# Low parts of decoded weights on VectorE, one-bank accumulators, and a later decode of one weight pair

## The chip, the cores and the metric

The kernel runs on one core of one Trainium2 chip. The metric is the device time of one execution in microseconds (us); lower is better. TensorE is called PE here, its weight loads PEld, VectorE DVE, ScalarE ACT, GpSimd POOL and SyncE, which issues the DMAs, SP. The times in the rows below count from the start of the span.

## The reference, cut to what matters

Three layers follow each other. The first is attention over a window of 64 positions (4 batches, 8 heads, 576 positions, 64 wide). The second mixes its output by a Fourier transform over positions and channels, normalises, and applies a two-layer network; the third is a gated network.

```python
X = np.fft.fft(np.fft.fft(x, axis=1), axis=2)
u = x + np.real(X)
un = (u - mean) / sqrt(var + 1e-6)
y = u + np.maximum(un @ w_ch1, 0) @ w_ch2          # 512 -> 2048 -> 512
h = gelu_tanh(y @ w_in); a, v = halves of h        # 512 -> 2 x 512
out = y + (a * (w_sg @ layernorm(v) + b_sg)) @ w_out
```

Everything is float32. The kernel multiplies in a faster format and keeps the precision by splitting each factor into a high and a low part: one product is three matmuls (`mm3`, L119 to L126: high by high, high by low, low by high).

## The kernel before, in words

**Decoding weights.** The weights arrive as raw 64-bit floats and are turned into float32 on the core, in pieces of 128x256. One piece (`raw`, L150 to L162) is a DMA on SP, one ACT instruction (L158, into `dec_g`) and three DVE instructions (L159, L160, L161, into `dec_w`). `halves` (L164 to L166) then splits a decoded piece: ACT copies the rounded value into the high part (L165), and POOL subtracts it from the piece to give the low part (L166). The parts go into one of nine buffers `set0` to `set8`. L166 runs 103 times in the program.

**The plain stage** (`mlp`, L636 to L683, about 156 to 350 us). The 2304 positions are cut into six chunks of 384, and the hidden layer into sixteen slices of 128. Six of the slices are computed plainly, in 36 blocks of one slice and one chunk. A block's first product gives `h` (12 matmuls, two buffers); ACT makes the high part of its ReLU, `rh` (L670), and DVE the low part, `rl` (L671). Two blocks later the second product (`second`, L642 to L657, 12 matmuls) adds into `acc`, one tile of four banks of PSUM. After a chunk's last slice four DVE additions (L656), one for each bank, move `acc` into the residual `uT`, and the next chunk takes the same tile.

**The seven-product stage** (`wino`, L870 to L912, about 348 to 588 us) computes the other ten slices, in pairs, by a scheme that needs seven products in place of eight. `decode_w1` (L180 to L204) decodes a pair's first weights and forms their sums and differences on DVE (L189, L194, L197, L202); `decode_w2` decodes its second weights. `tees(p)` (L694 to L726) forms the sums and differences of the activations and writes them to memory; `pump` loads them back. `quad` (L775 to L826) makes the seven products, each in a PSUM bank (`w`, six buffers, or `g`, two), and adds them up: DVE where a bank is read, POOL for two additions between SBUF tiles (`u<-u` and `u<-pq,u`, both L799). The two POOL additions stand before the DVE addition `pq<-w,pq`, which releases a bank. L792 (ACT) and L793 (DVE) make the ReLU's parts, and `units` (L828 to L857) does the second products, which L845 adds to `uT`. The first two products of the very first quad are issued early, inside the plain stage.

**What follows.** `split_x` (L864 to L868) splits the result into parts for the gated layer: 24 copies on ACT (L867) and 24 subtractions on POOL (L868).

**What sets the order.** The program is written as generators. `drive` takes work for PE from the main one and fills in pieces of side work from "lanes": decodes, norms, `tees`. A scheduler then places the instructions on each engine in an order of its own, by its own model of when each one could run, and an edit in one place can move instructions in many. Two helpers steer it. `high_priority(URGENT)` favours the instructions that release a bank. `behind(gen)` (L1178 to L1188) and the splitting at L1261 to L1265 place work after the instructions in `k.marks`, the last ReLU instructions named so far. `pair(6, G6)`, L1230, is the decode of the first pair of slices, 6 and 7; it is added to a lane when the second half of the chunks begins.

`k.bp` is the buffer pool of the plain and the seven-product stage. It is set in `open_mlp` (L622) and set to None at L1266.

Of the kernel before, what the change touches and what calls it, by code (L numbers as in the profile page):

```python
# [9 lines left out]
F32 = mybir.dt.float32  # L10
# [3 lines left out]
ALU = mybir.AluOpType  # L14
# [93 lines left out]
class Kernel:  # L108
# [54 lines left out]

    def halves(self, f, hi, lo):  # L164
        self.nc.scalar.activation(out=hi, in_=f, func=AF.Copy)  # L165
        self.nc.gpsimd.tensor_tensor(out=lo, in0=f, in1=hi, op=ALU.subtract)  # L166

    def decode(self, src, hi, lo, n=512):
        for o in range(0, n, 256):
# [466 lines left out]
    def mlp(self, before, last):  # L636
        nc = self.nc
        V, A = nc.vector, nc.scalar
        pend = []
        st = {}  # L640

        def second(g, n, f, rh, rl):  # L642
            t = self.sets[f % 8]
            start, size = CHUNKS[n]
            first, last = f == PHASES[g][0][0], f == PHASES[g][0][-1]
            if first:
                st["acc"] = self.bps.tile([128, 4, 512], F32, tag="acc", name="acc")
            acc = st["acc"]
            for c in range(4):
                s = slice(128 * c, 128 * c + 128)  # L650
                self.mm3(acc[:, c, 0:size], [(t[:, 2, s], t[:, 3, s], rh, rl)], first=first, last=last)
            if last:
                with self.tc.high_priority(URGENT):
                    for c in range(4):
                        x = self.uT[:, c, start:start + size]
                        v = V.tensor_tensor(out=x, in0=acc[:, c, 0:size], in1=x, op=ALU.add)  # L656
                self.marks = [v.ins]  # L657

        for g, (fs, ns) in enumerate(PHASES):
            for n in ns:  # L660
                before(g, n)
                xh, xl, size = self.xh[n], self.xl[n], CHUNKS[n][1]
                for f in fs:
                    t = self.sets[f % 8]
                    ps = self.bps.tile([128, 512], F32, tag="h", bufs=2, name="h")
                    o = ps[:, 0:size]
                    self.mm3(o, [(t[:, 0, 128 * k:128 * k + 128], t[:, 1, 128 * k:128 * k + 128], xh[:, k], xl[:, k]) for k in range(4)])
                    rh, rl = self.rpair(3)
                    with self.tc.high_priority(URGENT):
                        a = A.activation(out=rh, in_=o, func=AF.Relu)  # L670
                        v = V.scalar_tensor_tensor(out=rl, in0=o, scalar=0.0, in1=rh, op0=ALU.max, op1=ALU.subtract)  # L671
                        self.marks = [a.ins, v.ins]
                    pend.append((g, n, f, rh, rl))
                    yield 5 * size
                    if len(pend) > 2:
                        second(*pend.pop(0))
                        yield 5 * size
        while pend:
            second(*pend.pop(0))
            if last is not None:  # L680
                last()
                last = None
            yield 1500  # L683
# [91 lines left out]
    def quad(self, s, f, last, early=False):  # L775
# [2 lines left out]
        V, G, A = nc.vector, nc.gpsimd, nc.scalar  # L778
        self.nq += 1
        p1, p5, c11, u3 = self.ptiles[self.nq % 2], *self.ptiles[2:]  # L780
        out = {}

        def mm(i, o):
            hi, lo = self.w1_block(f, i)
# [5 lines left out]
        def relu(e, t, c, eng):  # L790
            rh, rl = self.rfree.pop(0)
            i = A.activation(out=rh, in_=c, func=AF.Relu)  # L792
            j = eng.scalar_tensor_tensor(out=rl, in0=c, scalar=0.0, in1=rh, op0=ALU.max, op1=ALU.subtract)  # L793
            out[e, t] = rh, rl
            return [i.ins, j.ins]

        hp = lambda: self.tc.high_priority(URGENT)
        copy = lambda o, i: A.activation(out=o, in_=i, func=AF.Copy)  # L798
# [1 line left out]
        for i in range(7):  # L800
            o = (self.gtile() if early and i < 2 else self.wps.tile([128, 512], F32, tag="w", name="w"))[:, 0:384]
            mm(i, o)
            with hp():
                if i == 0:
                    copy(p1, o)
                elif i == 1:
                    add(V, c11, o, p1)
                    relu(0, 0, c11, V)
                elif i == 2:
                    add(V, p1, o, p1)  # L810
                elif i == 3:
                    add(V, u3, o, p1)
                elif i == 4:
                    c21 = o
                elif i == 5:
                    copy(p5, o)
                    g = add(G, p1, p1, p5)
                    add(G, p5, u3, p5)
                    relu(1, 1, p5, V)
                    add(V, u3, c21, u3)  # L820
                    relu(1, 0, u3, V)
                else:
                    add(V, p1, o, p1)
                    self.marks = [*relu(0, 1, p1, V), g.ins]
            yield 960
        self.r[s, f] = out  # L826

# [250 lines left out]
def emit(tc, aps):  # L1078
    with ExitStack() as ctx:
# [142 lines left out]
        def before(g, n):  # L1222
            while n not in done:
                next(rest_)
            if n == PHASES[g][1][0]:
# [1 line left out]
                if g == 1:  # L1227
                    lanes[2].append(when(behind(blocks1()), lambda: 3 in done))
                elif g == 2:
                    lanes[1].append(pair(6, G6))  # L1230
                    lanes[2].append(behind(blocks()))
                elif g == 3:
                    drain(lanes[0], lanes[2])
                    lanes[1].append(pair(8, G8))
                    lanes[2].append(raws2())
# [107 lines left out]
```

## Time and profile before

| | before |
|---|---|
| median of 3 runs | 808.35 us (807.84 to 809.95) |
| profiled execution | 807.96 us, of which the span is 806.2 us |
| mean granted clock of TensorE | 0.979 |
| PE busy | 766.3 us (95%) |
| DVE busy | 526.2 us (65%) |
| ACT busy | 342.7 us (43%) |
| POOL busy | 288.5 us (36%) |

A busy time is the part of the span in which the engine worked on some instruction. "A <- B" in a row on waits means that an instruction of A stood still until B ended. The granted clock, PEclk, is a share of TensorE's full speed; 1.00 is 2.4 GHz, and 0.50 is 1.2 GHz.

### The profile page before, as it was taken

The numbers are of one execution on the slowest core, as the hardware profiler recorded it, in microseconds if no ns is written. First come the engines' busy times: TensorE is split into PE (matmuls) and PEld (weight loads), VectorE is DVE, ScalarE is ACT, GpSimd is POOL, SyncE is SP. The second block draws the span as 40 slices with busy tenths as digits, with TensorE's granted clock in tenths as the row PEclk, the third lists the DMA queues.
The fourth block names the chain that finished last, engine by engine and source line by source line (L and its number), as shares of the span: only waits on it lengthen the run. The fifth ranks groups of instructions, "written<-read, shape, count | busy, mean of one in ns | idle before, by whom it ended". The sixth has DMA issues, their size and how long they took to land.

```text
span 806.2 us, 13754 instructions
## 1 busy us (share of the span) xinstructions
PE 766.3 (95%) x5018; PEld 733.3 (91%) x5018; DVE 526.2 (65%) x1131; ACT 342.7 (43%) x807; POOL 288.5 (36%) x351
## 2 busy tenths in 40 slices
PE   7989699899999999979998999999899999999998
PEld 6879588798999989979998999999899998989898
DVE  4878959797377547885559866764760258674762
ACT  4877687664335544341224323331652243130310
POOL 2144535563433547245734412421692020010000
PEclk9999789999999999999999999999999999999999
DMA  8996662252205568538553970962240020204023
GB/s 263 333 266 181 178 192 73 70 168 83 100 27 188 193 218 296 192 127 337 192 221 115 354 288 5 388 249 110 72 136 1 1 67 1 80 11 147 1 79 117
DMA packets 84771, 123.36 MB, mean 153 GB/s; under 512 B 24416, under 2 KB 61664, under 8 KB 84704
## 3 DMA queue, kind: packets, MB, share of 16 engines
q1 hardware_dynamic: 82912, 119.13, 44.2%
q0 software_dynamic: 576, 2.97, 1.1%
q8 instruction: 39, 0.64, 0.3%
q10 hardware_dynamic: 1216, 0.39, 0.2%
q14 instruction: 28, 0.23, 0.1%
HBM read 91.79 MB, written 30.67 MB: 152 GB/s over the span
## 4 chain that ended last, share of the span: by engine, by line
PE 72%; DVE 14%; DMA 4%; ACT 4%; issue 3%; POOL 1%; SPq 0%; DVEq 0%; ACTq 0%; POOLq 0%
PE c L124 6%; PE c L125 6%; PE c L126 6%; PE g L124 6%; PE w L124 6%; PE g L126 5%; PE w L125 5%; PE w L126 5%; PE g L125 5%; PE sc L315 3%; DVE dec_w L160 2%; DVE dec_w L159 2%; PE acc L125 2%; PE acc L126 2%; PE h L124 2%
## 5 line engine op out<-in xcount | busy, mean ns | idle before, releaser
L166 POOL TENSOR_TENSOR set<-dec_w,set 128x256 fp32r<-128x256 f32 x103 | 82.9, 819 | 109.5 <-ACT set L165 86.2
L573 POOL TENSOR_TENSOR rq<-rq,mhalf 128x1 f32<-128x1 f32 (+1 forms) x24 | 16.8, 698 | 158.7 <-DVE rq L572 156.4
L158 ACT ACTIVATE dec_g<-dec_s 128x256 f32<-128x256 f32 x88 | 38.0, 436 | 69.6 <-DVE dec_w L160 31.1
L165 ACT ACTIVATE set<-dec_w 128x256 fp32r<-128x256 f32 x103 | 40.8, 413 | 62.4 <-DVE dec_w L161 29.8
L160 DVE SCALAR_TENSOR_TENSOR dec_w<-dec_g,dec_w 128x256 int32<-128x256 int32 x88 | 51.1, 584 | 1.9 <-ACT dec_g L158 0.6
L124 PE MATMUL acc<-rh,set 128*128 128x384 f32 x144 | 49.4, 343 | 2.7 <-DVE uT L656 1.7
L323 ACT ACTIVATE s<-s,mx 128x128 f32<-128x128 f32 x144 | 46.1, 391 | 11.0 <-DVE mx L321 10.9
L125 PE MATMUL acc<-rl,set 128*128 128x384 f32 x144 | 49.5, 344 | 0.0
L126 PE MATMUL acc<-rh,set 128*128 128x384 f32 x144 | 49.0, 340 | 0.0
L315 PE MATMUL sc<-k,q 128*128 128x128 f32 x288 | 41.9, 296 | 7.1 <-DVE s L318 4.0
L161 DVE SCALAR_TENSOR_TENSOR dec_w<-dec_s,dec_w 128x256 int32<-128x256 int32 x88 | 46.3, 532 | 0.4
L315 PEld LDWEIGHTS sc<-k,q 128*128 128x128 f32 x288 | 38.5, 209 | 8.5 <-DVE s L318 4.4
L159 DVE TENSOR_SCALAR dec_w<-dec_s 128x256 int32<-128x256 int32 x88 | 40.6, 467 | 7.1 <-DMA dec_s<-in_wo 2.8
L1004 DVE BATCH_NORM_STATS2 st<-u 128x6 f32<-128x512 f32 x18 | 12.4, 691 | 45.2 <-ACT u L1000 45.2
L799 DVE TENSOR_TENSOR u<-w,u 128x384 f32<-128x384 f32 x44 | 24.2, 550 | 26.6 <-POOL u L799 17.7
L318 DVE SCALAR_TENSOR_TENSOR s<-sc,mask 128x512 f32<-128x512 f32 x36 | 24.5, 683 | 25.3 <-PE pt L330 15.0
L799 POOL TENSOR_TENSOR u<-u 128x384 f32<-128x384 f32 x15 | 15.5, 1032 | 59.8 <-ACT u L798 42.1
L845 DVE TENSOR_TENSOR uT<-g,uT 128x384 f32<-128x384 f32 x36 | 19.2, 550 | 25.3 <-PE g L126 25.3
L656 DVE TENSOR_TENSOR uT<-acc,uT 128x384 f32<-128x384 f32 x48 | 23.4, 546 | 14.1 <-PE acc L126 14.0
L671 DVE SCALAR_TENSOR_TENSOR rl<-h,rh 128x384 fp32r<-128x384 f32 x36 | 19.6, 550 | 19.1 <-ACT rh L670 18.8
L343 PEld LDWEIGHTS pv<-v,pts 128*64 128x64 f32 x576 | 24.7, 148 | 7.3 <-issue 6.0
L124 PEld LDWEIGHTS acc<-rh,set 128*128 128x128 f32 x144 | 27.5, 191 | 4.0 <-DVE uT L656 2.4
(357 smaller groups left out, 2664.3 us busy)
## 6 DMA issues: line engine op xcount, KB each, us to landing
dec_s<-in_w SPq DMA_DIRECT2D x64, 256.0 KB, 2.8
v<-in_v SPq DMA_DIRECT2D x16, 520.0 KB, 5.2
xht<-xb SPq DMA_DIRECT2D x10, 768.0 KB, 8.1
xhm<-xb SPq DMA_DIRECT2D x10, 768.0 KB, 6.9
xlm<-xb SPq DMA_DIRECT2D x8, 768.0 KB, 8.1
k<-in_k SPq DMA_DIRECT2D x11, 512.0 KB, 6.7
xf<-u SPq DMA_DIRECT2D x18, 256.0 KB, 2.7
p<-xf SPq DMA_DIRECT2D x24, 192.0 KB, 2.7
```

The lines of the kernel that those rows point to most:

```text
L124: mm(out, lhsT=lh, rhs=rh, start=first and i == 0, stop=False)
L125: mm(out, lhsT=lh, rhs=rl, start=False, stop=False)
L126: mm(out, lhsT=ll, rhs=rh, start=False, stop=last and i == n - 1)
L158: nc.scalar.activation(out=g, in_=s[:, :, 1].bitcast(F32), func=AF.Copy, scale=2.0 ** -112)
L159: nc.vector.tensor_scalar(out=w, in0=s[:, :, 0], scalar1=29, scalar2=None, op0=ALU.logical_shift_right)
L160: nc.vector.scalar_tensor_tensor(out=w, in0=g[:].bitcast(I32), scalar=3, in1=w, op0=ALU.logical_shift_left, op1=ALU.bitwise_or)
L161: nc.vector.scalar_tensor_tensor(out=w, in0=s[:, :, 1], scalar=-2147483648, in1=w, op0=ALU.bitwise_and, op1=ALU.bitwise_or)
L165: self.nc.scalar.activation(out=hi, in_=f, func=AF.Copy)
L166: self.nc.gpsimd.tensor_tensor(out=lo, in0=f, in1=hi, op=ALU.subtract)
L315: nc.tensor.matmul(sc[:, hp], lhsT=q[:, hp].rearrange("p a b -> p (a b)"), rhs=k[:, hp, o:o + 128], start=True, stop=True)
L323: nc.scalar.activation(out=s[:, hp], in_=s[:, hp], func=AF.Exp, bias=mx[:, hp:hp + 1])
L799: add = lambda eng, o, i, j: eng.tensor_tensor(out=o, in0=i, in1=j, op=ALU.add)
```

## The change

It has four parts, and the line numbers here are those of before.

1. **Low parts** (L166): where `self.bp` is set, the subtraction is issued on DVE and not on POOL. That holds for 83 of the 103; the other 20 (12 during attention, 8 at the end) stay.
2. **Banks** (L647 to L656): `acc` becomes four tiles of one bank each, with a tag each, `acc0` to `acc3`. The second product's groups and the four additions use one tile each, in place of a quarter of one.
3. **Marks of a quad** (L781 to L824): `self.marks` after a quad names the instructions of all four ReLUs and the first POOL addition. Before, it named those of the last ReLU that is written and that addition. `tees(2)` (L1251) and `split_x` (L1261) are placed behind these marks.
4. **Pair 6** (L1230): its decode goes through `behind`, so that each of its steps is placed after the marks that stand when it is first taken.

```diff
--- before.py
+++ after.py
@@ -163,7 +163,7 @@
 
     def halves(self, f, hi, lo):
         self.nc.scalar.activation(out=hi, in_=f, func=AF.Copy)
-        self.nc.gpsimd.tensor_tensor(out=lo, in0=f, in1=hi, op=ALU.subtract)
+        (self.nc.gpsimd if self.bp is None else self.nc.vector).tensor_tensor(out=lo, in0=f, in1=hi, op=ALU.subtract)
 
     def decode(self, src, hi, lo, n=512):
         for o in range(0, n, 256):
@@ -644,16 +644,16 @@
             start, size = CHUNKS[n]
             first, last = f == PHASES[g][0][0], f == PHASES[g][0][-1]
             if first:
-                st["acc"] = self.bps.tile([128, 4, 512], F32, tag="acc", name="acc")
+                st["acc"] = [self.bps.tile([128, 512], F32, tag=f"acc{c}", name="acc") for c in range(4)]
             acc = st["acc"]
             for c in range(4):
                 s = slice(128 * c, 128 * c + 128)
-                self.mm3(acc[:, c, 0:size], [(t[:, 2, s], t[:, 3, s], rh, rl)], first=first, last=last)
+                self.mm3(acc[c][:, 0:size], [(t[:, 2, s], t[:, 3, s], rh, rl)], first=first, last=last)
             if last:
                 with self.tc.high_priority(URGENT):
                     for c in range(4):
                         x = self.uT[:, c, start:start + size]
-                        v = V.tensor_tensor(out=x, in0=acc[:, c, 0:size], in1=x, op=ALU.add)
+                        v = V.tensor_tensor(out=x, in0=acc[c][:, 0:size], in1=x, op=ALU.add)
                 self.marks = [v.ins]
 
         for g, (fs, ns) in enumerate(PHASES):
@@ -778,7 +778,7 @@
         V, G, A = nc.vector, nc.gpsimd, nc.scalar
         self.nq += 1
         p1, p5, c11, u3 = self.ptiles[self.nq % 2], *self.ptiles[2:]
-        out = {}
+        out, marks = {}, []
 
         def mm(i, o):
             hi, lo = self.w1_block(f, i)
@@ -792,7 +792,7 @@
             i = A.activation(out=rh, in_=c, func=AF.Relu)
             j = eng.scalar_tensor_tensor(out=rl, in0=c, scalar=0.0, in1=rh, op0=ALU.max, op1=ALU.subtract)
             out[e, t] = rh, rl
-            return [i.ins, j.ins]
+            marks.extend((i.ins, j.ins))
 
         hp = lambda: self.tc.high_priority(URGENT)
         copy = lambda o, i: A.activation(out=o, in_=i, func=AF.Copy)
@@ -814,14 +814,15 @@
                     c21 = o
                 elif i == 5:
                     copy(p5, o)
-                    g = add(G, p1, p1, p5)
+                    marks.append(add(G, p1, p1, p5).ins)
                     add(G, p5, u3, p5)
                     relu(1, 1, p5, V)
                     add(V, u3, c21, u3)
                     relu(1, 0, u3, V)
                 else:
                     add(V, p1, o, p1)
-                    self.marks = [*relu(0, 1, p1, V), g.ins]
+                    relu(0, 1, p1, V)
+                    self.marks = marks
             yield 960
         self.r[s, f] = out
 
@@ -1227,7 +1228,7 @@
                 if g == 1:
                     lanes[2].append(when(behind(blocks1()), lambda: 3 in done))
                 elif g == 2:
-                    lanes[1].append(pair(6, G6))
+                    lanes[1].append(behind(pair(6, G6)))
                     lanes[2].append(behind(blocks()))
                 elif g == 3:
                     drain(lanes[0], lanes[2])
```

With `order` the two programs can be laid side by side. In the changed program lines from L784 on stand one or two lower, so L868 there is L867 here.

**DVE at the end of the plain stage.** These are the last four additions that empty the accumulator, and what stands ahead of them. Before:

```order
L159 TENSOR_SCALAR dec_w_4751<-dec_s_4748 128x256
L161 SCALAR_TENSOR_TENSOR dec_w_4714<-dec_s_4711,dec_w_4714 128x256
L160 SCALAR_TENSOR_TENSOR dec_w_4751<-dec_g_4750,dec_w_4751 128x256
L159 TENSOR_SCALAR dec_w_4777<-dec_s_4774 128x256
L161 SCALAR_TENSOR_TENSOR dec_w_4751<-dec_s_4748,dec_w_4751 128x256
L160 SCALAR_TENSOR_TENSOR dec_w_4777<-dec_g_4776,dec_w_4777 128x256
L656 TENSOR_TENSOR uT_61<-acc_4182,uT_61 128x384 x4
L161 SCALAR_TENSOR_TENSOR dec_w_4777<-dec_s_4774,dec_w_4777 128x256
L159 TENSOR_SCALAR dec_w_4957<-dec_s_4954 128x256
```

After:

```order
L656 TENSOR_TENSOR uT_61<-acc_4170,uT_61 128x384
L656 TENSOR_TENSOR uT_61<-acc_4171,uT_61 128x384
L189 TENSOR_TENSOR dec_w_4648<-dec_w_4618,dec_w_4641 128x256
L166 TENSOR_TENSOR set5_2054<-dec_w_4641,set5_2054 128x256
L656 TENSOR_TENSOR uT_61<-acc_4215,uT_61 128x384
L656 TENSOR_TENSOR uT_61<-acc_4216,uT_61 128x384
L166 TENSOR_TENSOR set5_2054<-dec_w_4648,set5_2054 128x256
L159 TENSOR_SCALAR dec_w_4674<-dec_s_4671 128x256
L656 TENSOR_TENSOR uT_61<-acc_4217,uT_61 128x384
L160 SCALAR_TENSOR_TENSOR dec_w_4674<-dec_g_4673,dec_w_4674 128x256
L656 TENSOR_TENSOR uT_61<-acc_4218,uT_61 128x384
L161 SCALAR_TENSOR_TENSOR dec_w_4674<-dec_s_4671,dec_w_4674 128x256
```

The four additions stood in one piece behind ten decode steps of pair 8. Now each bank's addition is an instruction with its own release, and one or two steps of a decode, low parts among them, stand between the pairs. In the whole program pair 6's decode moved on DVE from blocks 3 to 17 to blocks 25 to 30 (two of its first steps stay in block 5), and pair 8's from blocks 17 to 35 to blocks 31 to 35. From the 24th L671 to the last L656 the three lines L159 to L161 stand 54 times where they stood 38 times, the sums and differences L189 to L202 9 times where they stood 6 times, and L166 24 times where it did not stand. The early products of the first quad moved by three blocks or more on PE: the first from before block 26 to before block 29.

**POOL in the seven-product stage,** around the two additions of a quad. Before, in the sixth quad:

```order
L166 TENSOR_TENSOR set2_71<-dec_w_5199,set2_71 128x256
L799 TENSOR_TENSOR u_4195<-u_4195,u_4197 128x384
L166 TENSOR_TENSOR set1_70<-dec_w_5245,set1_70 128x256
L166 TENSOR_TENSOR set1_70<-dec_w_5142,set1_70 128x256
L166 TENSOR_TENSOR set1_70<-dec_w_5192,set1_70 128x256
L799 TENSOR_TENSOR u_4197<-pq_4199,u_4197 128x384
L166 TENSOR_TENSOR set1_70<-dec_w_5285,set1_70 128x256
L166 TENSOR_TENSOR set2_71<-dec_w_5199,set2_71 128x256
```

After, from the fifth quad to the start of the sixth:

```order
L720 TENSOR_TENSOR p_4482<-p_4482,po_4498 128x384
L719 CAST po_4503<-p_4478 128x384
L720 TENSOR_TENSOR p_4478<-p_4478,po_4503 128x384
L799 TENSOR_TENSOR u_4232<-u_4232,u_4233 128x384
L799 TENSOR_TENSOR u_4233<-pq_4235,u_4233 128x384
L799 TENSOR_TENSOR u_4231<-u_4231,u_4233 128x384
```

Low parts stood between the two additions of a quad. Now the second addition follows the first, and the last subtractions of `tees(2)` (L720) stand behind the fourth quad's additions; they stood between them.

**ACT at the end of the seven-product stage:** the last ReLU copies (L792) and the splitting. Before:

```order
L165 ACTIVATE set8_2989<-dec_w_6743 128x256
L165 ACTIVATE set8_2989<-dec_w_6753 128x256
L792 ACTIVATE xht_2985<-u_4196 128x384
L867 ACTIVATE xh0_119<-uT_61 128x384 x4
L867 ACTIVATE xhm_2050<-uT_61 128x384 x8
L867 ACTIVATE xht_2985<-uT_61 128x384 x2
L792 ACTIVATE rh0_2061<-u_4197 128x384
L867 ACTIVATE xht_2985<-uT_61 128x384
L792 ACTIVATE xlt_2986<-pq_4199 128x384
```

After:

```order
L798 ACTIVATE u_4233<-w_6487 128x384
L158 ACTIVATE dec_g_6788<-dec_s_6786 128x256
L165 ACTIVATE set8_2998<-dec_w_6779 128x256
L792 ACTIVATE xht_2994<-u_4232 128x384
L165 ACTIVATE set8_2998<-dec_w_6789 128x256
L792 ACTIVATE rh0_2061<-u_4233 128x384
L792 ACTIVATE xlt_2995<-pq_4235 128x384
L868 ACTIVATE xh0_119<-uT_61 128x384 x4
```

Fourteen of the copies L867 stood ahead of the last but one ReLU copy. Now all copies (L868 there) stand behind the last one.

## Rows read from the trace of the kernel before

**Rows 1.** Page, first part: busy time, share of the span, instructions of each engine

```profile
PE 766.3 (95%) x5018; PEld 733.3 (91%) x5018; DVE 526.2 (65%) x1131; ACT 342.7 (43%) x807; POOL 288.5 (36%) x351
```

**Rows 2.** Waits of PE from 140 us on: us in total, times, longest

```profile
PE h L124 <- DVE rl L671: 4.3, 3, 2.2
PE w L124 <- DVE uT L656: 3.2, 1, 3.2
PE w L124 <- DVE pq L799: 2.6, 1, 2.6
PE w L124 <- ACT rh L792: 2.0, 1, 2.0
PE acc L124 <- DVE uT L656: 1.7, 2, 1.5
PE g L591 <- ACT bs L510: 1.5, 1, 1.5
PE g L124 <- DVE pl L514: 1.4, 1, 1.4
PE acc L124 <- ACT rh L670: 1.0, 2, 0.7
```

**Rows 3.** Busy by stretch: us, PE, PEld, DVE, ACT, POOL, PEclk, DMA share, GB/s

```profile
140.00:195.00 55.00, 48.54 (x335) 45.48 (x334) 49.13 (x100) 32.71 (x76) 30.21 (x35) 0.97 0.35 111
285.80:352.30 66.50, 61.77 (x347) 61.00 (x347) 44.58 (x93) 28.47 (x65) 29.60 (x33) 0.97 0.61 209
442.00:575.00 133.00, 132.88 (x763) 132.31 (x762) 93.06 (x201) 43.90 (x103) 38.25 (x43) 1.00 0.59 223
```

**Rows 4.** The same view of a short stretch right behind a wait

```profile
352.00:355.20 3.20, 2.85 (x9) 2.86 (x10) 3.20 (x9) 0.86 (x2) 0.81 (x1) 0.50 0.27 97
```

**Rows 5.** Timeline of DVE, 347 to 353 us: start us, us, instruction, count

```profile
348.41 0.82 DVE L159 TENSOR_SCALAR dec_w<-dec_s 128x256 int32<-128x256 int32 x1
349.15 0.94 DVE L161 SCALAR_TENSOR_TENSOR dec_w<-dec_s,dec_w 128x256 int32<-128x256 int32 x1
...
350.35 1.94 DVE L656 TENSOR_TENSOR uT<-acc,uT 128x384 f32<-128x384 f32 x4
```

**Rows 6.** Timeline of POOL in the same place

```profile
348.12 1.69 POOL L166 TENSOR_TENSOR set<-dec_w,set 128x256 fp32r<-128x256 f32 x2 [0.46 <-PE acc L125]
```

**Rows 7.** All runs of three decode lines: duration ns min/median/max, first and last start

```profile
L159 DVE TENSOR_SCALAR dec_w<-dec_s x88: 231/286/1396, 27.2 to 592.9; 128x256 int32<-128x256 int32 x88
...
L160 DVE SCALAR_TENSOR_TENSOR dec_w<-dec_g,dec_w x88: 386/417/1534, 28.2 to 594.6; 128x256 int32<-128x256 int32 x88
...
L960 DVE TENSOR_TENSOR set<-dec_s,set x7: 411/425/629, 570.1 to 662.3; 128x256 fp32r<-128x256 f32 x4, 128x320 fp32r<-128x320 f32 x3
```

**Rows 8.** Timeline of POOL, 425 to 440 us

```profile
431.50 1.20 POOL L799 TENSOR_TENSOR u<-u 128x384 f32<-128x384 f32 x1
432.66 2.18 POOL L166 TENSOR_TENSOR set<-dec_w,set 128x256 fp32r<-128x256 f32 x3
434.81 1.19 POOL L799 TENSOR_TENSOR u<-pq,u 128x384 f32<-128x384 f32 x1
```

**Rows 9.** Timeline of DVE, 430 to 440 us

```profile
438.42 0.55 DVE L799 TENSOR_TENSOR pq<-w,pq 128x384 f32<-128x384 f32 x1
```

**Rows 10.** Timeline of ACT, 574 to 606 us

```profile
578.12 3.40 ACT L867 ACTIVATE xhm<-uT 128x384 fp32r<-128x384 f32 x8
...
582.26 0.51 ACT L792 ACTIVATE rh<-u 128x384 fp32r<-128x384 f32 x1
```

**Rows 11.** Groups by line, POOL, 285 to 355 us: busy, mean, idle before

```profile
L166 POOL TENSOR_TENSOR set<-dec_w,set 128x256 fp32r<-128x256 f32 x22 | 17.8, 825 | 24.3 <-ACT set L165 13.2 <-PE h L125 10.3 <-PE acc L125 0.8
```

**Rows 12.** The same view, 355 to 588 us

```profile
L166 POOL TENSOR_TENSOR set<-dec_w,set 128x256 fp32r<-128x256 f32 x42 | 34.0, 822 | 65.2 <-ACT set L165 53.2 <-PE w L126 5.9 <-PE g L125 5.5
```

**Rows 13.** Timeline of POOL, 355 to 432 us: the third block set's last subtractions

```profile
397.50 1.99 POOL L720 TENSOR_TENSOR p<-p,po 128x384 fp32r<-128x384 f32 x2
...
419.73 1.06 POOL L799 TENSOR_TENSOR u<-u 128x384 f32<-128x384 f32 x1
```

## The prediction

> **What bounds the kernel now.** I read the busy shares first: PE works through 95% of the span [rows 1], so the time is PE's work plus the stretches in which it stands or runs slowly. The next view is PE's waits. From 140 us on, where the change acts, the waits listed come to 17.7 us [rows 2]; behind them are DVE (L671, L656, L799, L514) or ACT (L670, L792, L510), never a DMA. The third view shows where these two are short of time: in 140 to 195 us DVE is busy for 49.13 of 55.00 us and PE for 48.54, so a DVE busy for 89% of a stretch goes with 6.5 us of PE standing still, while in 442 to 575 us a DVE busy for 70% leaves PE at 132.88 of 133.00 [rows 3]. The fourth view is the granted clock. Right behind the wait that ends at 352 us the clock is 0.50 for 3.2 us [rows 4], PE's 1.2 GHz level; half of that, 1.6 us, is lost work. Four such windows stand in the trace from 140 us on, behind the waits at 157, 285, 349 and 581 us. A wait that goes can take its window along.
>
> Why DVE is late is seen at the largest wait, 349 us. The additions L656 that release the accumulator stand behind an L159 that took 0.82 us and an L161 that took 0.94 [rows 5], while POOL did two L166 [rows 6]. The median L159 takes 0.286 us, the median L160 0.417, and the longest 1.40 and 1.53 [rows 7]. Operations between SBUF tiles are slow on DVE when POOL is at work.
>
> **The low parts.** 83 subtractions leave POOL, at 0.82 us each there [rows 11, 12]. The nearest operation on DVE has the same form, a subtraction for a high and a low part in L960, and takes a median of 0.425 us [rows 7]: 83 x 0.425 = 35 us more for DVE. Against that stands what the meetings with POOL cost: 0.53 us each for the L159 and the L161 in [rows 5]. If each low part on POOL slows between a half and nine tenths of such a step today, 83 of them give back 22 to 40 us. DVE's total then hardly changes, and lies anywhere from 5 us below to 13 us above. That is not on PE's path as a whole; what counts is the stretches that are full.
>
> **The banks.** The two waits for L656, of 1.7 and 3.2 us, come to 4.9 us in [rows 2], 4.7 of them in the two largest; all four additions (1.94 us, [rows 5]) had to end before one tile was free. With a tile for each bank PE needs only the first addition, and three more matmul groups of three, some 1.6 us, stand behind the bank that it finishes first. One addition takes 0.5 us, so it is covered unless DVE is late by a microsecond. I take 4.4 us for both waits and 1.6 us for the clock window behind the second. The bounds are 0 (DVE is late anyway) and 6.3.
>
> **POOL between a quad's additions.** In the sixth quad three L166, 2.18 us together, stand between `u<-u` and `u<-pq,u` [rows 8], and DVE's `pq<-w,pq`, which PE waits for, comes at 438.42 [rows 9]. After the change nothing stands between. I take 2.3 of the 2.6 us; the bounds are 0, if the DVE steps that stood ahead of it stay, and 2.6. The other quads wait for nothing here that PE shows.
>
> **The marks.** At the end of the seven-product stage the ReLU copy that PE waits for starts at 582.26, behind the split copies, of which eight take 3.40 us [rows 10]. In the new order no split copy stands ahead of it: 2.0 us [rows 2], and 1.6 us for the window behind it. The copies themselves start some 5 us later; the gated layer reads the first of them only after the 96 matmuls of the last second products, so they stay hidden at no cost. For `tees(2)`, its last subtractions end at 399.5 us, and the quad that reads them has its first POOL addition at 419.73 [rows 13]; they move behind one more POOL addition of some 1.2 us, so I cost that at nothing too, with most of these 20 us as cover.
>
> **Pair 6's decode.** It leaves blocks 3 to 17, where DVE is at 89% [rows 3]. Of the two waits at 179 and 182 us (1.5 and 1.4 us, [rows 2]) I take 1.5. At 157 us DVE's order ahead of the late L671 is the same, and only three matmuls more stand ahead of the waiting one: 0.5 of 2.2 us, and the window stays. The waits at 263, 284 and 285 us (2.8 us in the rows of L671 and L670, [rows 2]) stand behind additions, norms and copies rather than behind low parts; I take 0.7. Its eight loads on SP come later too, behind those of `tees(0)`; they are not waited for today and cost nothing.
>
> It arrives in the last third of the plain stage, and this is the price. From 285.8 to 352.3 us DVE is busy for 44.58 of 66.5 us [rows 3]. The new order puts 24 low parts (10.2 us), 16 more steps of L159 to L161 (about 0.38 us, 6.1 us) and 3 more sums (1.3 us) there: 62.2 us. The 22 low parts that POOL does there [rows 11] no longer slow DVE; at 0.53 us for half to two thirds of them that gives back 6 or 7, so about 55 to 57 us. The stretch itself loses its two waits of 4.7 us and one window of 1.6 us, and is then 60 us long. DVE would be at 92 to 95% there. The row for such a load is 140 to 195 us: 6.5 us of waiting at 89%, and a window. Against it speaks that a low ReLU part is needed only two blocks later, 24 matmuls or 4 us, so that short delays vanish. Between nothing and 8 us I take 4, and 1 us for the seven-product stage, whose DVE gains load from a lower level.
>
> **The sum.** 4.4 + 1.6 + 2.3 + 2.0 + 1.6 + 1.5 + 0.5 + 0.7 = 14.6 us of gain, less 5.0: 9.6 us. The profiled execution's 807.96 becomes 798.4; the median of the runs before lies 0.4 higher, so I say **798.7**.
>
> **A rule against it.** What the rows show is a DVE step of 0.29 us at 0.82 while POOL subtracts [rows 5, 6], and L960, which like the moved low part reads two SBUF tiles, between 0.411 and 0.629 us [rows 7]. The Trainium skill, page "SBUF — State Buffer", section "Who interferes with whom", states that a DVE instruction with two SBUF inputs and a GpSimd instruction that reads SBUF exclude each other, and that the one that comes second is blocked until the first is done. By that rule, and the trace agrees, the moved subtraction stays a party to the conflict with what POOL keeps.
>
> **The rivals.**
>
> *The conflict only moves.* POOL keeps about 12 of its 29.6 us in the full stretch (29.60 less the 17.8 us of L166, [rows 3, 11]), and the two additions of every quad, 1.2 us each [rows 8]. If low parts on DVE lengthen these as much as the decode steps were lengthened, half of the gain at 436 us (1.2) and the gain at 179 us (1.5) are lost, and 2 to 3 us more in the full stretch: 804. The longest L960, 0.629 us, speaks against it, since it lost 0.2 us and not 0.5.
>
> *DVE becomes the bound; slower than before.* In its own queue a low part that waits holds up L671 and L656. POOL's low parts waited 13.2 us for ACT and 10.3 us for PE in the full stretch [rows 11], and 11.4 us for PE later [rows 12]; nobody stood behind them. If the 10.3 us come on top of 57 us, and 12 us of POOL's remaining work slow a part of the new steps by 6 us, DVE needs 73 us for the stretch of 60. That is 13 us and another window of 1.6, and the 6.0 us of the banks don't come: 8.6 - 14.6 is a loss of 6.0, so 814. It decides from some 71 us in this stretch on; below that the gains elsewhere keep the kernel at or below its time. Against it: the order was made with the waits in view, and 4 us of lead on PE absorb single waits.
>
> *Gaps only move.* The waits shown go, but as many return at other places in the new order, with two of their clock windows: 14.6 less 13 gives 807.
>
> *DVE keeps up everywhere.* No new waits: 14.6 us, and half of those that I left at 179 to 182 and 263 to 285 us, 1.7: 792.
>
> **How the numbers follow.** The forecast, 796 to 802, gets 0.45; the moved conflict 0.15, DVE keeping up 0.12, gaps that only move 0.13, DVE as the bound 0.15. 0.3% (2.4 us, about what a measurement can tell from no change) is beaten by the first three, 0.72; the fourth lies within it, 0.13; the last is slower, 0.15. The range runs from 791.0 to 809.5 and leaves out the slower case and a little on either side.
>
> **What would show it.** In the profile after, L159 and L160 should have means near their medians, and no wait for `uT` L656 over half a microsecond should stand at 342 to 352 us. `rh` L792 and `pq` L799 should be gone from PE's waits, with the half-clock windows at 352 and 584 us. If DVE is busy for over 95% from block 24 to the last L656, and PE waits for `rl` L671 there, the price was too low; if L166 on DVE has a mean over 0.6 us, the conflict moved. The forecast is wrong if PE's waits from 140 us on still come to over 15 us, or if new ones name a low part.

## The result and the profile after

The changed kernel takes 794.83 us (median of 4 runs, 793.43 to 796.32); the kernel before, timed beside it, takes 808.23. The ratio is 0.9827 with a 95% interval of 0.9809 to 0.9844, so 13.4 us are gone. The profiled execution took 794.30 us, with a span of 792.5.

The first part of the page answers [rows 1]:

```profile
PE 760.9 (96%) x5018; PEld 728.0 (92%) x5018; DVE 538.2 (68%) x1214; ACT 341.9 (43%) x807; POOL 225.2 (28%) x268
```

DVE has 83 instructions more and is busy for only 12.0 us more; POOL is busy for 63.3 us less. PE is busy for 5.4 us less with the same matmuls, and four half-clock windows are gone, two of them ahead of 140 us (at 14 and 51 us).

The waits of PE from 140 us on, in the order of [rows 2]:

```profile
PE w L124 <- DVE u L799: 2.2, 2, 1.7
PE w L124 <- DVE pq L799: 1.8, 1, 1.8
PE h L124 <- DVE rl L671: 1.7, 1, 1.7
PE acc L124 <- DVE uT L656: 1.5, 1, 1.5
PE w L124 <- DMA xl<-xb: 0.7, 1, 0.7
...
PE w L124 <- DVE uT L656: 0.6, 1, 0.6
...
PE w L124 <- DMA xht<-xb: 0.4, 1, 0.4
```

Of the waits in [rows 2] those behind `rh` L792 (581 us), `pq` L799 at 436 us, `pl` L514 and `bs` L510 are gone. `w` behind L656 fell from 3.2 to 0.6 us. The first two rows here are new: they stand at 348, 350 and 353 us, and come to 3.9 us. The wait of `acc` stands at 297 us, also a new place. The two DMA waits, at 402 and 411 us, are for blocks that `tees(2)` made.

The busy times by stretch, as in [rows 3] (the same work, earlier by what was saved so far), and a window at half clock:

```profile
137.90:192.90 55.00, 52.14 (x359) 49.34 (x356) 46.49 (x106) 31.94 (x73) 21.23 (x23) 0.97 0.31 96
277.20:341.70 64.50, 62.39 (x360) 61.38 (x359) 59.40 (x141) 31.39 (x76) 13.24 (x11) 1.00 0.65 222
...
356.30:359.50 3.20, 3.20 (x12) 3.20 (x12) 3.20 (x10) 1.17 (x3) 0.00 (x0) 0.50 1.03 421
```

In the last third of the plain stage DVE is busy for 59.40 of 64.50 us, 92%, and PE still works for 62.39. From 140 us on two half-clock windows are left, at 158 and at 356 us; before there were four.

All runs of three lines, in answer to [rows 7]:

```profile
L159 DVE TENSOR_SCALAR dec_w<-dec_s x88: 233/283/1399, 24.5 to 580.9; 128x256 int32<-128x256 int32 x88
...
L160 DVE SCALAR_TENSOR_TENSOR dec_w<-dec_g,dec_w x88: 384/415/1483, 26.0 to 583.6; 128x256 int32<-128x256 int32 x88
...
L166 DVE TENSOR_TENSOR set<-dec_w,set x83: 403/412/1541, 158.3 to 551.9; 128x256 fp32r<-128x256 f32 x83
```

The medians are as before and the longest ones too. What has fallen is the number of meetings. Of the 228 runs of L159 to L161 between 150 and 600 us, 102 overlap an instruction of POOL in the trace before and 55 after. No run without such an overlap took over 0.43 us in either trace; those with one took 0.73 us in the mean before and 0.83 after. The groups by line show what that does to the means. These are the decode lines before:

```profile
L160 DVE SCALAR_TENSOR_TENSOR dec_w<-dec_g,dec_w 128x256 int32<-128x256 int32 x88 | 51.1, 584 | 1.9 <-ACT dec_g L158 0.6
...
L161 DVE SCALAR_TENSOR_TENSOR dec_w<-dec_s,dec_w 128x256 int32<-128x256 int32 x88 | 46.3, 532 | 0.4
...
L159 DVE TENSOR_SCALAR dec_w<-dec_s 128x256 int32<-128x256 int32 x88 | 40.6, 467 | 7.1 <-DMA dec_s<-in_wo 2.8 <-POOL set L166 2.6 <-DMA dec_s<-in_w 0.7
```

And after (us busy, then mean ns behind the bar):

```profile
L160 DVE SCALAR_TENSOR_TENSOR dec_w<-dec_g,dec_w 128x256 int32<-128x256 int32 x88 | 46.5, 535 | 2.6 <-ACT dec_g L158 2.2
L161 DVE SCALAR_TENSOR_TENSOR dec_w<-dec_s,dec_w 128x256 int32<-128x256 int32 x88 | 43.8, 506 | 0.3
L166 DVE TENSOR_TENSOR set<-dec_w,set 128x256 fp32r<-128x256 f32 x83 | 37.5, 459 | 7.5 <-ACT set L165 7.3
L159 DVE TENSOR_SCALAR dec_w<-dec_s 128x256 int32<-128x256 int32 x88 | 35.8, 411 | 6.0 <-DMA dec_s<-in_w 3.2 <-DMA dec_s<-in_wo 2.1 <-DMA dec_s<-in_wi 0.3
```

**A measure that leaves the start out.** In the traces of all kernels here the first matmul into `acc` starts between 154.3 and 158.1 us, also where nothing ahead of it was changed; before it starts at 157.1 and after at 155.1, so 2.0 us of the difference between these two traces are of that kind. The stretch from that matmul to the first one of the gated layer (`c<-xh`) holds the plain and the seven-product stage. It is called the middle below: 435.9 us before (157.1 to 593.0), 423.4 after (155.1 to 578.5). 12.5 us came from there. The waits of over 0.15 us in it went from 18.4 to 9.6 us, and two half-clock windows fewer, at 1.6 us each, make up nearly all the rest. Each kernel has one trace, and a window is partly chance: every trace has a wait of 1.7 or 2.2 us between 154 and 161 us, and in two of the fourteen (without marks, pair 6 early) no window follows it. A difference of one window between two kernels says little.

### The profile page after: what moved, and what is told of

It is laid out like the page before. It is cut to its first block, busy times and chain, and to the rows that moved or that the text cites. A ratio compares the mean times of both kernels' runs of the same rounds, so it can differ in the third digit from the quotient of the medians.

```text
span 792.5 us, 13690 instructions
## 1 busy us (share of the span) xinstructions
PE 760.9 (96%) x5018; PEld 728.0 (92%) x5018; DVE 538.2 (68%) x1214; ACT 341.9 (43%) x807; POOL 225.2 (28%) x268
## 5 line engine op out<-in xcount | busy, mean ns | idle before, releaser
L799 POOL TENSOR_TENSOR u<-u 128x384 f32<-128x384 f32 x15 | 17.5, 1166 | 185.5 <-ACT u L798 160.1
L124 PE MATMUL acc<-rh,set 128*128 128x384 f32 x144 | 47.5, 340 | 1.7 <-DVE uT L656 1.5
L126 PE MATMUL acc<-rh,set 128*128 128x384 f32 x144 | 48.3, 337 | 0.0
L160 DVE SCALAR_TENSOR_TENSOR dec_w<-dec_g,dec_w 128x256 int32<-128x256 int32 x88 | 46.5, 535 | 2.6 <-ACT dec_g L158 2.2
L315 PE MATMUL sc<-k,q 128*128 128x128 f32 x288 | 40.1, 288 | 5.4 <-DVE s L318 4.0
L161 DVE SCALAR_TENSOR_TENSOR dec_w<-dec_s,dec_w 128x256 int32<-128x256 int32 x88 | 43.8, 506 | 0.3
L315 PEld LDWEIGHTS sc<-k,q 128*128 128x128 f32 x288 | 36.8, 201 | 6.8 <-DVE s L318 4.4
L166 DVE TENSOR_TENSOR set<-dec_w,set 128x256 fp32r<-128x256 f32 x83 | 37.5, 459 | 7.5 <-ACT set L165 7.3
L799 DVE TENSOR_TENSOR u<-w,u 128x384 f32<-128x384 f32 x44 | 24.2, 550 | 23.8 <-POOL u L799 19.5
L159 DVE TENSOR_SCALAR dec_w<-dec_s 128x256 int32<-128x256 int32 x88 | 35.8, 411 | 6.0 <-DMA dec_s<-in_w 3.2
L671 DVE SCALAR_TENSOR_TENSOR rl<-h,rh 128x384 fp32r<-128x384 f32 x36 | 19.7, 547 | 22.7 <-ACT rh L670 22.7
L343 PE MATMUL pv<-v,pts 128*64 128x65 f32 x576 | 29.6, 237 | 2.1 <-DMA v<-in_v 1.7
L846 DVE TENSOR_TENSOR uT<-g,uT 128x384 f32<-128x384 f32 x36 | 19.5, 551 | 16.9 <-PE g L126 16.7
L798 ACT ACTIVATE u<-w 128x384 f32<-128x384 f32 x29 | 14.1, 487 | 37.0 <-PE w L126 36.6
```

Source lines behind the costliest of these rows:

```text
L124: mm(out, lhsT=lh, rhs=rh, start=first and i == 0, stop=False)
L126: mm(out, lhsT=ll, rhs=rh, start=False, stop=last and i == n - 1)
L160: nc.vector.scalar_tensor_tensor(out=w, in0=g[:].bitcast(I32), scalar=3, in1=w, op0=ALU.logical_shift_left, op1=ALU.bitwise_or)
L161: nc.vector.scalar_tensor_tensor(out=w, in0=s[:, :, 1], scalar=-2147483648, in1=w, op0=ALU.bitwise_and, op1=ALU.bitwise_or)
L166: (self.nc.gpsimd if self.bp is None else self.nc.vector).tensor_tensor(out=lo, in0=f, in1=hi, op=ALU.subtract)
L315: nc.tensor.matmul(sc[:, hp], lhsT=q[:, hp].rearrange("p a b -> p (a b)"), rhs=k[:, hp, o:o + 128], start=True, stop=True)
```

## The experiments

Two theories were set against each other. A: POOL's subtractions slow VectorE's decode steps wherever the two meet, and that is most of what the change takes away. B: each part of the change removes the wait at its own place. Where a kernel is called "alone" or "without", its edit against the kernel before is a subset of the diff above.

| kernel | time, us | ratio to before, 95% interval | middle, us |
|---|---|---|---|
| before | 808.2 to 809.4 | | 435.9 |
| changed | 794.83 | 0.9827 (0.9809 to 0.9844) | 423.4 |
| low parts alone | 793.20 | 0.9805 (0.9756 to 0.9853) | 424.1 |
| banks alone | 802.52 | 0.9917 (0.9890 to 0.9944) | 431.5 |
| marks alone | 807.91 | 0.9988 (0.9965 to 1.0010) | 435.6 |
| pair 6 alone | 811.63 | 1.0027 (1.0002 to 1.0052) | 442.2 |
| without low parts | 807.88 | 0.9996 (0.9971 to 1.0021) | 435.8 |
| without banks | 797.53 | 0.9865 (0.9828 to 0.9901) | 426.0 |
| without marks | 798.21 | 0.9867 (0.9830 to 0.9903) | 429.0 |
| pair 6 early | 797.40 | 0.9860 (0.9813 to 0.9907) | 422.9 |
| idle subtractions | 801.87 | 0.9913 (0.9887 to 0.9938) | 431.7 |
| half on POOL | 799.98 | 0.9899 (0.9870 to 0.9928) | 428.6 |
| differences on DVE | 788.73 | 0.9759 (0.9736 to 0.9781) | 417.0 |
| low parts, differences | 795.53 | 0.9833 (0.9804 to 0.9861) | 424.2 |

### Each part alone

**Low parts alone:**

```diff
-        self.nc.gpsimd.tensor_tensor(out=lo, in0=f, in1=hi, op=ALU.subtract)
+        (self.nc.gpsimd if self.bp is None else self.nc.vector).tensor_tensor(out=lo, in0=f, in1=hi, op=ALU.subtract)
```

> The kernel before with the 83 low parts on VectorE and nothing else changed. Theory A (what cost time was POOL's subtraction slowing decode steps on VectorE wherever they met): the means of L159 and L160 fall towards their medians, the waits at 179, 182 and 436 us shrink to under half, the waits at 342 and 349 us to about half, and the time is 800 to 803. Theory B (each part of the change removes the wait at its own place, and the low parts only the one at 436 us): 805 to 806. Rival C (low parts in VectorE's queue delay L671 and L656): 808 to 812.

It took 793.20 us, below every range named: one line gives the whole gain. Three of the four half-clock windows from 140 us on are gone with it. PE's waits at 179, 182 and 436 us are gone from its trace, though pair 6's decode is as early as before. The waits for L656, with the accumulator still one tile of four banks, fell from 4.9 to 2.9 us:

```profile
PE acc L124 <- DVE uT L656: 1.5, 2, 1.0
PE w L124 <- DVE uT L656: 1.4, 1, 1.4
```

**Banks alone:**

```diff
-                st["acc"] = self.bps.tile([128, 4, 512], F32, tag="acc", name="acc")
+                st["acc"] = [self.bps.tile([128, 512], F32, tag=f"acc{c}", name="acc") for c in range(4)]
```

> The kernel before with the accumulator as four tiles of one bank and nothing else changed. Theory B: the waits for L656 at 342 and 349 us (4.7 us) fall to about 0.6 us and the half-clock window behind goes: 802 to 803. Theory A: VectorE is still late by 0.5 us in each slowed decode step, so that one or two microseconds stay, with the window: 804.5 to 806.5.

It took 802.52 us, as theory B said, and the waits for L656 fell to 0.7 us. But 2.8 us of new waits stand right behind, at 354 to 362 us, for the first quads' additions on DVE and ACT. And the 2.6 us wait at 436 us is gone too, though the low parts are still on POOL; three others, 2.3 us in all, stand at 426 to 437 us. So the agreement with theory B's time is partly luck.

**Marks alone:**

```diff
-                    self.marks = [*relu(0, 1, p1, V), g.ins]
+                    relu(0, 1, p1, V)
+                    self.marks = marks
```

> The kernel before with the marks of a quad naming all its ReLUs and nothing else changed. Theories A and B alike: the wait for rh L792 at 581 us (2.0 us) and the half-clock window behind it (1.6 us) go, the rest stays: 804 to 805. If the order elsewhere moves with it and chance reordering is worth microseconds by itself, the time lies outside 803 to 806.

It took 807.91 us, no difference that can be told, and not the 804 to 805 of both theories. It lies where the expectation put a reordering that is worth microseconds by itself. The edit did what it says: in its trace ACT makes the last ReLU copies first (starts in us, then duration):

```profile
577.39 0.53 ACT L792 ACTIVATE rh<-u 128x384 fp32r<-128x384 f32 x1 [0.26 <-POOL u L799]
...
579.02 0.52 ACT L792 ACTIVATE xlt<-pq 128x384 fp32r<-128x384 f32 x1
579.46 1.75 ACT L868 ACTIVATE xh<-uT 128x384 fp32r<-128x384 f32 x4
```

The wait then moved to DVE, whose steps meet POOL's splitting subtractions a little later in the same place:

```profile
580.26 1.24 DVE L160 SCALAR_TENSOR_TENSOR dec_w<-dec_g,dec_w 128x256 int32<-128x256 int32 x1
581.42 1.35 DVE L793 SCALAR_TENSOR_TENSOR xlt<-pq,xlt 128x384 fp32r<-128x384 f32 x1
```

PE waited 1.4 us for that L793 and 1.5 us for a late L846, in place of 2.0 and 0.6.

**Pair 6 alone:**

```diff
-                    lanes[1].append(pair(6, G6))
+                    lanes[1].append(behind(pair(6, G6)))
```

> The kernel before with pair 6's decode placed behind the marks and nothing else changed; low parts on POOL. Theory B: the waits at 179 and 182 us (2.9 us) go, and the last third of the plain stage gets new ones of 2 to 4 us: 806 to 809. Theory A: decode steps and POOL's low parts now crowd in the last third, so it costs more than it gives: 809 to 813.

It took 811.63 us; the middle is 6.3 us longer. The waits at 263, 284 and 285 us are gone with the window behind them. But those at 179 and 182 us fell by 0.7 us only, and the last third of the plain stage got dearer: `acc` waits 2.9 us for L656 at 342 us, `h` 2.1 us for L671 at 300 us, each with a half-clock window twice as long as those before. With low parts on POOL theory A's price for the crowd is right.

### The change less one part

**Without low parts:** L166 as before, the rest as changed.

> The changed kernel with the low parts back on POOL; banks, marks and pair 6 as changed. Theory A (POOL's subtraction slowing VectorE is most of the cost): little of the gain is left, 802 to 808, with waits for L656, L671 or L799 in the last third of the plain stage above 5 us. Theory B (each part its own place): 797 to 799.

It took 807.88 us: the three other parts together give nothing. Theory B falls with this run. PE waits 3.4 us for L656 ahead of `acc`, 2.8 for L671 and 3.2 for L799 in its trace.

**Without banks:** one tile of four banks, the rest as changed.

> The changed kernel with the accumulator again as one tile of four banks. Theory B: the waits for L656 between chunks and before the first quad come back with about 4 us, 798.5 to 800. Theory A: VectorE is no longer slowed there, the four additions come in time but for 1 to 2 us: 796 to 798.

It took 797.53 us, within theory A's range, and the middle is 2.6 us longer than in the changed kernel. Ahead of the last two changes of the accumulator, at 335 and 341 us, PE waits 2.0 us for L656 in place of 0.6, and a half-clock window stands at 297 us.

**Without marks:** `self.marks` as before, the rest as changed.

> The changed kernel with the marks of a quad as before. Theories A and B alike: the split copies stand ahead of a ReLU copy again, 2.0 us of waiting and a half-clock window of 1.6 us come back at the end of the seven-product stage: 797.5 to 799.

It took 798.21 us, the middle 5.6 us longer. At the end of the seven-product stage 3.0 us of waits and a half-clock window came back. The two waits on DMAs stayed, at 403 and 412 us, with 1.5 us. So the marks, worth nothing on their own, take off some 3 us of waits once the low parts are off POOL. How much time that is worth is less sure, for the intervals of the two ratios still overlap a little.

**Pair 6 early:** `pair(6, G6)` without `behind`, the rest as changed.

> The changed kernel with pair 6's decode as early as before. Theory B: 2.9 us of waits at 179 and 182 us come back, 797 to 798, and the new waits of 3.9 us at 348 to 353 us stay. Theory A: the early decode no longer meets low parts on POOL, the last third is emptier, and the waits at 297 and 348 to 353 us shrink: 790 to 795.

It took 797.40 us, theory B's number, but not by its mechanism. The interval of its ratio overlaps that of the changed kernel. Its middle, 422.9 us, is no longer than that of the changed kernel; the difference stands ahead of and behind it, where the two programs do the same. The wait at 179 us stayed short (0.5 us), against theory B, and 3.6 us of waits at 351 to 355 us stayed, as theory B said and against theory A. Whether the pair is early or late hardly matters once the low parts are on DVE.

### What POOL does to VectorE

**Idle subtractions:**

```diff
+        if self.bp is not None:
+            for c in range(0, 256, 64):
+                self.nc.gpsimd.tensor_tensor(out=self.junk, in0=hi[:, c:c + 64], in1=hi[:, c:c + 64], op=ALU.subtract)
```

> The changed kernel, low parts on VectorE, and after each high part POOL also subtracts it from itself in four pieces of 128x64, into a scrap tile nobody reads: POOL's traffic is back, but nothing waits for it. The conflict theory (POOL's reading of SBUF slows VectorE's steps, whatever it computes): means of L159 and L160 rise to 0.45 and 0.57 us or more, the moved L166 to 0.55 or more, and the time is 800 to 807. The rival (what counted was that a low part on POOL came late and kept its buffer, a matter of who waits for whom): 794 to 797, means unchanged.

It took 801.87 us: 7.0 us of the 13.4 are lost when POOL does work whose results nobody reads. The groups by line (L161 is L160 of the changed kernel here, L160 is L159, L167 is L166):

```profile
L161 DVE SCALAR_TENSOR_TENSOR dec_w<-dec_g,dec_w 128x256 int32<-128x256 int32 x88 | 52.2, 598 | 0.7
...
L167 DVE TENSOR_TENSOR set<-dec_w,set 128x256 fp32r<-128x256 f32 x83 | 41.1, 500 | 4.1 <-ACT set L166 3.7 <-PE g L125 0.4
...
L160 DVE TENSOR_SCALAR dec_w<-dec_s 128x256 int32<-128x256 int32 x88 | 38.1, 438 | 6.1 <-DMA dec_s<-in_wo 4.2 <-DMA dec_s<-in_w 1.8
...
L170 POOL TENSOR_TENSOR junk<-set 128x64 f32<-128x64 f32 x332 | 125.2, 377 | 66.7 <-ACT set L166 43.8
```

POOL is busy with them for 125 us, where the 83 low parts at 0.82 us would take 68, so this is more than the old traffic. The means rose to 0.598, 0.500 and 0.438 us from 0.535, 0.459 and 0.411; two of them stayed a little under what the conflict theory had named. DVE waits for none of these POOL instructions, so the rival, a late low part that keeps its buffer, doesn't explain this loss. The instructions were again placed anew by the scheduler, so a part of the 7.0 us may be order.

The other half of the gain stays open. Take what L159 to L161 lose between 150 and 600 us against runs without an overlap: 37 us before, 25 in the changed kernel, 36 here. That loss is back almost whole, and the time is not. Single delays are shorter here, 0.55 us in the mean of the runs beside POOL, where it was 0.73 before. And before, DVE stood still seven times for an L166 of POOL (`dec_w` L197 and L159), 6.1 us in all, so the rival may hold for a part.

The Trainium skill, page "SBUF — State Buffer", section "Who interferes with whom", has POOL's reads as the reason, and by it a DVE addition with one of its two inputs in PSUM is not blocked. The traces agree: L656 is such an addition, and before, its 26 runs beside POOL have a mean of 0.545 us and the other 22 one of 0.547.

**Half on POOL:**

```diff
+        self.nlow += self.bp is not None
-        (self.nc.gpsimd if self.bp is None else self.nc.vector).tensor_tensor(...)
+        (self.nc.gpsimd if self.bp is None or self.nlow % 2 else self.nc.vector).tensor_tensor(...)
```

> The changed kernel with every second of the 83 low parts back on POOL. If the cost goes with the number of meetings on VectorE: about half-way between 794.8 and the 807.9 of all on POOL, 800 to 803. If VectorE was too full with all 83, and POOL free enough for half of them: 792 to 796.

It took 799.98 us, 5 us above all on DVE and 8 us below all on POOL. POOL had time for half of them and it still cost. The meetings lie between as well: 83 of 227 runs of L159 to L161 overlap an instruction of POOL, where it was 55 of 228 in the changed kernel and 114 in the one without low parts on DVE.

### The waits that came new

In the changed kernel DVE does this at 344 us, where nothing but decodes and first quads is due:

```profile
344.56 1.23 DVE L166 TENSOR_TENSOR set<-dec_w,set 128x256 fp32r<-128x256 f32 x1
345.71 1.24 DVE L160 SCALAR_TENSOR_TENSOR dec_w<-dec_g,dec_w 128x256 int32<-128x256 int32 x1
346.87 1.24 DVE L166 TENSOR_TENSOR set<-dec_w,set 128x256 fp32r<-128x256 f32 x1
348.04 0.55 DVE L799 TENSOR_TENSOR u<-w,u 128x384 f32<-128x384 f32 x1
```

And POOL, without a break:

```profile
343.29 1.20 POOL L799 TENSOR_TENSOR u<-u 128x384 f32<-128x384 f32 x1 [40.92 <-ACT u L798]
344.45 1.06 POOL L706 TENSOR_TENSOR p<-p 128x384 f32<-128x384 f32 x1
345.47 1.20 POOL L799 TENSOR_TENSOR u<-pq,u 128x384 f32<-128x384 f32 x1
346.63 3.70 POOL L706 TENSOR_TENSOR p<-p 128x384 f32<-128x384 f32 x3
```

**Differences on DVE:**

```diff
-            sub = lambda o, a, b: (G if p == 2 else V).tensor_tensor(out=f[o], in0=f[a], in1=f[b], op=ALU.subtract)
+            sub = lambda o, a, b: V.tensor_tensor(out=f[o], in0=f[a], in1=f[b], op=ALU.subtract)
```

> The changed kernel with the eight differences of the third block set (L706, on POOL today, 1.0 us each) on VectorE. The conflict theory: the new waits at 348 to 353 us (3.9 us, where L166 and L160 take 1.2 us beside these differences) fall under 1.5 us and their half-clock window goes: 790 to 793. The rival (VectorE is full there by itself): the waits stay or grow, 794 to 798.

It took 788.73 us, 6.1 us less than the changed kernel, and is the fastest kernel here. The stretch from 341 to 357 us in the changed kernel (columns as in [rows 3]):

```profile
341.00:357.00 16.00, 12.06 (x64) 10.78 (x63) 15.97 (x28) 6.55 (x16) 10.15 (x10) 0.98 0.73 256
```

And in this one:

```profile
341.00:357.00 16.00, 15.81 (x91) 15.49 (x90) 15.12 (x38) 7.13 (x18) 5.65 (x3) 1.00 0.83 308
```

DVE is full in both. But with POOL at 5.65 us in place of 10.15 it got through 38 instructions in place of 28, and PE worked for 15.81 us in place of 12.06. Of its 5.65 us, 3.2 are one L799 that starts at 353.81, beside which DVE's steps take their ordinary 0.29 to 0.56 us. The time is 1.3 us below the conflict theory's range. Of the waits 0.9 us are left, at 357 us, and one of 1.3 us for L793 stands at 361 us, so the 1.5 us named for them are not quite kept. The window at 356 us is gone, and so are the DMA waits at 402 and 411 us.

**Low parts, differences:** the same edit, on top of the low parts alone.

> The kernel before with the 83 low parts and the eight differences of the third block set on VectorE; banks, marks and pair 6 as before. The low parts alone gave 793.2. The conflict theory: POOL's last 8.6 us beside the decodes go, 791 to 793. The rival (no wait of PE stood there in that order, so nothing to gain): 793 to 795.

It took 795.53 us, and its middle is 424.2 us against 424.1: no gain, and both ranges missed. In that order PE had waited only 0.9 us at this place, for L793 at 357 us. That wait is gone, and with it 1.5 us of waits in all, but one half-clock window more, at 578 us, takes them back.

## Why the prediction was right, and where its steps were not

The forecast was 798.7 us with a range from 791.0 to 809.5; it came to 794.83, better by 3.9. It missed the 796 to 802 that had the largest chance and lies between them and the 792 of "DVE keeps up everywhere". The direction and its ground, that POOL slows DVE, hold; that the size came so near is partly luck, as the steps show. By its own steps:

**The low parts.** 83 of them were to cost 35 us on DVE and to change its total by -5 to 13 us. They cost 37.5 us, and the total rose by 12.0, so 25.5 came back, of the 22 to 40 named: right. Of these, 11.9 us lie in L159 to L161. But the means of L159 and L160, which were to come near their medians, went less than a third of the way (L159 from 0.467 to 0.411 us, with a median of 0.283). And somebody did stand behind POOL's low parts: DVE, for 6.1 us. That this was worth little as a whole and mattered only in full stretches was the frame in which I gave the low parts just the wait at 436 us. That is the step that failed. The runs show low parts alone giving all of the gain, and the three other parts nothing without them. The sum gave each wait to the edit that stands nearest to it, as if the edits added up.

**The banks.** 4.4 us and a window were taken; the waits for L656 at these two places fell from 4.7 to 0.6 us, 4.1. A window still follows, at 356 us, now behind the new waits. And half of the 4.1 us comes without the banks: with low parts alone the same waits are 2.4 us at 335 and 342 us.

**POOL between a quad's additions.** 2.3 us were taken, 2.6 came. That the low parts between the additions were the cause is not shown: the wait at 436 us is gone with the banks alone and with pair 6 alone too, where others of 1.9 to 2.3 us in all stand between 426 and 445 us. With the low parts alone nothing stands there.

**The marks.** 2.0 us and a window were taken and came. That no cost stands behind was right for the copies, but only with the low parts off POOL: alone, the marks moved the wait to DVE. The two waits on DMAs for the blocks of `tees(2)`, 1.1 us, are not the price of its marks, which I had put at nothing: without the marks these waits come to 1.5 us. They are gone with the differences on DVE; which part of the change makes them stays open.

**Pair 6's decode.** Its waits at 179 and 182 us went entirely (2.9 us, 1.5 taken), but not by the move: they are gone with pair 6 early too but for 0.5 us, and the move alone took off 0.7. At 157 us 0.5 us went, as said, but by the banks: this wait is 1.7 us in every trace with one-bank accumulators and 2.2 in every other. At 263, 284 and 285 us I took 0.7 of 2.8; all went, and the window at 287 us with them. That is the move's own work, sized too small: no trace with a late pair 6 has a wait of over 0.15 us from 255 to 290 us, pair 6 alone among them. Every trace with an early one has 0.7 to 2.9 us there, with low parts alone 0.4 and 0.3.

**The price of a full stretch.** DVE was to be at 92 to 95% in the last third of the plain stage and is at 92%. The price of 4 us there was too high: waits of 1.5 us at 297 and 0.6 at 338 are all. But right behind, at 348 to 353 us, stand 3.9 us and a window of 1.6 us, where the sum had 1 us for the whole seven-product stage. The place was wrong, and the ground was not the load: with the differences on DVE it is busy for 15.12 of 16.00 us there, where it was 15.97, and PE hardly waits.

**The rivals.** "The conflict only moves" was half true: at that place it does, though the mean of a moved L166 is 0.459 us and not over 0.6: 15 of the 83 overlap an instruction of POOL and take 0.66 us in the mean, the other 68 take 0.41. "DVE becomes the bound" did not come; 71 us were needed, and DVE had 59.40 of 64.50. The two profiled executions are 13.7 us apart where the sum had 9.6. Of these 4.1 us, 2.0 stand ahead of the middle, where nothing was changed, and the part behind it took 0.9 longer. The middle gave 2.9 more than the sum. The larger differences are 2.1 at 263 to 285 us and 1.6 for the window there, 1.4 at 179 and 182, less 3.1 for the new waits and their window (8.1 in place of 5); they come to 2.0. The other 0.9 us lie in smaller ones and are not told apart here. So the sum came near because terms that were too small and a price that was too small cancel in part.

## What to carry to other kernels

Where VectorE and GpSimd both work between SBUF tiles, look at the mean against the median of VectorE's short instructions, and count the meetings before the busy shares: an operation can be cheaper on the fuller of the two engines, as the low parts were here (0.82 us on POOL, 0.46 on DVE). Don't add up the edits of a change as if each owned the waits nearest to it; an edit that moves work out of the way pays only once the engine that is waited for can use the room. And when the load of an engine seems to bound a stretch, compare how many instructions it gets through there.

## What the runs showed of the hardware

At 344 us of the changed kernel, where both engines have work in a row, a VectorE step of 0.41 us takes 1.23 to 1.24 us, three in a row at starts 1.15 and 1.16 us apart, while GpSimd's additions of 1.02 us take 1.20. In some 1.16 us each engine gets through one instruction, where the two alone add up to 1.43; so they run nearly one after the other. I had expected a slowdown of 0.53 us for a step, as in [rows 5]; back to back it is 0.82.

It is not always VectorE that loses: with the differences on DVE one GpSimd addition of 1.02 us took 3.22, and the steps beside it were not slowed.

VectorE's steps on SBUF tiles alone were never slow without GpSimd: in the trace before, the 126 runs of L159 to L161 from 150 to 600 us that overlap no GpSimd instruction took at most 0.43 us, and the longest of the 102 others took 1.53.
